# Reading K and V of a decode attention in tiles of four heads instead of two, on one core

## The chip, the core and the metric

The kernel runs on one core of a Trainium2 chip. Its time is the device time of one execution in microseconds (us). TensorE (PE) multiplies matrices, VectorE (DVE), ScalarE (ACT) and GpSimd (POOL) work on elements, SyncE (SP) issues the transfers, and 16 DMA engines carry them from HBM into the 128 partitions of SBUF. PSUM holds TensorE's results, in eight banks of 512 f32 columns.

## The reference

One decode step of one layer for B = 4 sequences with one new token each, model width D = 576, 32 query heads over 16 K/V heads of 128 features, and a window of the last 4096 positions of a cache of 16384:

```python
def _A_ref(x, k_cache, v_cache, wq, wo):
    W = min(4096, max(256, Sk // 4))            # 4096
    rep = Hq // Hkv                             # 2
    q = (x @ wq).reshape(B, Sq, Hq, Dh).transpose(0, 2, 1, 3)
    k = jnp.repeat(k_cache[:, :, Sk - W:, :], rep, axis=1)
    v = jnp.repeat(v_cache[:, :, Sk - W:, :], rep, axis=1)
    p = _softmax(jnp.einsum("bhqd,bhkd->bhqk", q, k) * (Dh ** -0.5), axis=-1)
    o = jnp.einsum("bhqk,bhkd->bhqd", p, v)
    return o.transpose(0, 2, 1, 3).reshape(B, Sq, Hq * Dh) @ wo

h = x + _A_ref(_layernorm(x), A_k_cache, A_v_cache, A_wq, A_wo)
h2 = h + _B_ref(_layernorm(h), B_W_gate, B_W_up, B_W_down)   # relu(x Wg) * (x Wu) @ Wd, F = 4608
```

All inputs are bf16. The windows of K and V are 134 MB of the 159.6 MB that the kernel reads.

## The kernel before

Each engine has a program of its own, written out in order by hand: `prog_sync` (SP's transfers), `prog_pool`, `prog_act`, `prog_dve`, `prog_pe`. `S.op` and `S.dma` add an instruction with the names that it waits for (`deps`) and the name that it signals. An engine takes its instructions strictly in the order of its program, so an instruction that waits holds up all behind it.

**Tiles.** K and V come as "duos": two heads of one sequence, 4096 positions each, 16 KB a partition, 2 MB. Partition 2p + s holds 64 positions of head s. There are 32 duos of K and 32 of V. `add` gives each transfer a place in `pool` and makes it wait for the last reader of what lay there. K has four slots, freed by the second transpose of a duo (`TR`), V has four, freed by its product (`PV`). The order of the transfers is Wq, five duos of K, then K and V in turn (`VLEAD` = 5), Wo, W_gate, W_up, W_down. `pool` is reused for the weights behind: Wo in K's slots, W_gate and W_up where the last V duos lay, W_down in place of Wo, once `ATTN` (the product with Wo) is done.

**Scores.** DVE transposes each half duo in 32 x 32 blocks of f32 words, two bf16 at a time (`tr`, L414), from `pool` into `kT`, a ring of three halves. TensorE (`qk`, all its matmuls have the helper's line L518) multiplies it with `qz`, a query matrix that is zero except for the rows of one duo. Four duos make a batch: their scores add up in the same four banks `sc`, 16 query rows in each of four groups of 32 partitions. Columns alternate between the two heads of a duo, so half of the scores belong to the wrong head.

**Softmax.** After a batch's last score DVE takes the maximum (`rmax`, L417), POOL reduces it over partitions (L293), DVE makes two biases (`fbias`, L425 to L429), one for each head position; for rows of the wrong head the bias is so low that the exponential is 0. ACT takes the exponentials (L342), one instruction for each half and head position, into `P`. DVE transposes `P` (`trp`, L433), ACT casts it to bf16 `prob` (L349).

**Values.** TensorE multiplies `prob` with V (`pv`) into a bank for the batch, ACT copies the bank (`cpy`, L327), TensorE picks the diagonal blocks (`ext`) and DVE divides by the sums (`norm`). `pv` runs five duos behind `qk`.

**Order on DVE.** All transposes of K in turn; after the eighth half of a batch the maximum and the biases; then the first transpose of the next batch, and only then `trp` of this batch. `qk` of the next batch waits for the exponentials (`EXP`), since there is only one set of banks.

The rest (projection of q, Wo, the second layer norm, the gated feed-forward part) is as before and after.

Of the kernel before, what the change touches and what calls it, by code (L numbers as in the profile page):

```python
# [12 lines left out]
B = 4  # L13
# [6 lines left out]
T = WIN // 64  # L20
# [3 lines left out]
NDUO = B * KVH // 2  # L24
NB = 4
NBATCH = NDUO // NB
NHB = 4 * NB
# [3 lines left out]
DUO = 2 * WIN * DH // 128  # L31
NKS = 4
NVS = 4
# [3 lines left out]
NKT = 3  # L37
VLEAD = 5
PVLAG = 5
# [63 lines left out]
def bass_sequential_preLN__sliding_block_cached__glu_gated_reglu__decode_kernel(  # L103
# [12 lines left out]
    with ExitStack() as es:  # L116
# [4 lines left out]

        pool = sb("pool", [128, (NKS + NVS) * DUO], BF16)
        kT = sb("kT", [128, NKT, DUO // 4], FP32)
# [6 lines left out]
        x_f = sb("x_f", [B, D], FP32)  # L130
        junk_f = sb("junk_f", [B, D], FP32)
# [12 lines left out]
        qz = sb("qz", [128, 2, NB, 4, 128], BF16)  # L144
        mask = sb("mask", [128, 3, NHB], FP32)
        selT = sb("selT", [128, 4, NHB], FP32)
        rmx = sb("rmx", [128, 2, 2], FP32)
        rsel = sb("rsel", [128, 2], FP32)
# [4 lines left out]
        bias = sb("bias", [128, 2, 2], FP32)  # L153
        rs2 = sb("rs2", [128, 2, 4], FP32)
        rs1 = sb("rs1", [128, 2], FP32)
        P = sb("P", [128, T * 32], FP32)
        probT = sb("probT", [128, T, 32], FP32)
        prob = sb("prob", [128, 2, NB, T, 4], BF16)
# [12 lines left out]
        hhT = probT[:, 0:FC // 2, :].bitcast(BF16).rearrange("p f b -> p (f b)")[:, 0:FC * 32].rearrange("p (f b) -> p f b", b=32)  # L171
        S8 = probT[:, FC // 2:FC // 2 + 16, :].bitcast(BF16).rearrange("p f b -> p (f b)")
# [39 lines left out]
        def duo(cache, d):  # L212
            b, m = divmod(d, KVH // 2)
            return cache[b, 2 * m:2 * m + 2, SK - WIN:SK, :].rearrange("s (p t) d -> p s (t d)", p=64)

        def add_K(d):
            s = d % NKS
            add(("K", d), f"kslot{s}", s * DUO, DUO, ("TR", 2 * d + 1),
                lambda e, o: e.dma_start(out=o, in_=duo(A_k_cache, d)))

        def add_V(d):
            s = d % NVS
            add(("V", d), f"vslot{s}", (NKS + s) * DUO, DUO, ("PV", d),
                lambda e, o: e.dma_start(out=o, in_=duo(A_v_cache, d)))
# [3 lines left out]
        add(("wq", 0), "wq0", NKS * DUO, 4 * HQ, "QMM",  # L228
            lambda e, o: e.dma_start(out=o, in_=A_wq[0:512, :].rearrange("(p u) n -> p (u n)", u=4)))
        add(("wq", 4), "wq4", NKS * DUO + 4 * HQ, HQ // 2, "QMM",  # L230
            lambda e, o: e.dma_start(out=o, in_=A_wq[512:576, :].rearrange("r (u n) -> (r u) n", u=2)))
        for m in range(NDUO + VLEAD):
            if m < NDUO:
                add_K(m)
            if m >= VLEAD:
                add_V(m - VLEAD)
# [60 lines left out]
        def prog_act(S):  # L297
# [12 lines left out]
            def qzero(n):  # L310
                b, q = divmod(n, 2)
                for g in range(4):
                    deps = []
                    if g == 0:
                        deps = ["D_QR", "QZ0"] if n < 2 else [("QK", 2 * NB * (n - 1) - 1)]
                    src = bass.AP(tensor=qrep, offset=32 * g * 4 * H * B + NHB * q * B + b,
                                  ap=[[4 * H * B, 32], [4 * B, NB], [H * B, 4], [B, 4]])
                    dst = bass.AP(tensor=qz, offset=32 * g * 2 * NB * 512 + (n % 2) * NB * 512 + 32 * g,
                                  ap=[[2 * NB * 512, 32], [512 + 4, NB], [128, 4], [1, 4]])
                    S.op(a, lambda e, src=src, dst=dst: e.copy(out=dst, in_=src), deps=deps,  # L320
                         name=("QZ", n) if g == 3 else None, signal=g == 3)

            def cpy(n):
                deps = [("PV", NB * n + NB - 1)]
                if n >= 2:
                    deps.append(("EXT", n - 2))
# [4 lines left out]
            for n in range(NBATCH):  # L331
# [19 lines left out]
                if n >= 1:  # L351
                    cpy(n - 1)
# [352 lines left out]
```

## Time and profile before

| | before |
|---|---|
| median of the runs (3) | 382.47 us (382.41 to 382.47) |
| the profiled execution: time, span of its instructions | 382.39 us, 381.1 us |
| read from HBM | 159.58 MB, 419 GB/s over the span |
| DMA engines busy | 98.8% of the span |
| PE, DVE, ACT busy | 284.2, 206.3, 53.5 us |
| granted TensorE clock, mean | 0.909 |

A line of a group reads: line, engine, operation, output <- input, partitions x elements and type, count; then busy us and mean ns of one; then the idle time ahead of it and what ended that. A line of a timeline begins with the start and the length in us; several neighbours of a kind are merged, with their count. Durations hold the first to the last element; instructions of an engine can overlap a little.

### The profile page before, as it was taken

How to read it: one execution, taken by the hardware profiler on the slowest of the kernel's cores; microseconds unless marked ns; L12 is line 12 of the kernel's file. 1: busy time of each engine (PE TensorE's matmuls, PEld its weight loads, DVE VectorE, ACT ScalarE, POOL GpSimd, SP SyncE). 2: the span in 40 equal slices, each digit the busy share in tenths (PEclk: the TensorE clock that was granted, in tenths of full speed). 3: DMA queues.
4: the chain of work that ended last, by engine and by line, in shares of the span. 5: the costliest groups of instructions: out<-in, count | busy, mean ns of one | idle time of the engine just before them, and what ended most of it. 6: DMA issues, size and time to landing. Idle time of an engine off the chain costs nothing.

```text
span 381.1 us, 3911 instructions
## 1 busy us (share of the span) xinstructions
PE 284.2 (75%) x1701; PEld 124.4 (33%) x1716; DVE 206.3 (54%) x193; ACT 53.5 (14%) x129; POOL 8.2 (2%) x22
## 2 busy tenths in 40 slices
PE   0059749976996699669957995799779996945474
PEld 0053213322432243224322432243224333435341
DVE  0259789369447754774487548644775443042021
ACT  4012050021102110211031103100310021010020
POOL 4100000000000000000000000000000000000000
PEclk9999969998999899989998999899859997975669
DMA  8999999999999999999999999999999999999995
GB/s 331 409 430 428 426 435 420 434 423 428 431 423 433 423 430 425 428 430 426 430 426 428 430 426 425 432 425 430 426 428 432 421 433 420 420 444 432 414 411 227
DMA packets 11985, 159.84 MB, mean 419 GB/s; under 512 B 1336, under 2 KB 1472, under 8 KB 2624
## 3 DMA queue, kind: packets, MB, share of 16 engines
q1 hardware_dynamic: 11960, 159.59, 98.8%
q8 instruction: 13, 0.21, 0.2%
q14 instruction: 4, 0.03, 0.0%
q10 hardware_dynamic: 8, 0.00, 0.0%
HBM read 159.58 MB, written 0.00 MB: 419 GB/s over the span
## 4 chain that ended last, share of the span: by engine, by line
DMA 34%; PE 33%; DVE 20%; issue 5%; ACT 5%; SPq 1%; POOL 1%; POOLq 0%
DMA pool<-in_A_k_cache_dram 27%; PE pb L518 17%; PE sc L518 16%; DVE kT L414 11%; DMA pool<-in_B_W_down_dram 7%; ACT P L342 4%; DVE probT L433 3%; DVE rmx L417 3%; SPq L254 1%; POOL bcm L293 1%; DVE P L475 1%; DVE P L471 0%; DVE bias L429 0%; DVE sel L374 0%; ACT cp L327 0%
## 5 line engine op out<-in xcount | busy, mean ns | idle before, releaser
L414 DVE STREAM_TRANSPOSE kT<-pool 128x2048 f32<-128x2048 f32 x64 | 144.2, 2290 | 55.8 <-DMA pool<-in_A_k_cache_dram 52.9
L518 PE MATMUL sc<-kT,qz 128*128 128x512 bf16 x497 | 132.1, 418 | 50.2 <-DVE kT L414 46.7
L518 PE MATMUL pb<-pool,prob 128*16 128x512 bf16 x512 | 116.5, 388 | 0.0
L518 PEld LDWEIGHTS sc<-kT,qz 128*128 128x128 bf16 x512 | 48.6, 101 | 130.7 <-DVE kT L414 57.6
L518 PEld LDWEIGHTS pb<-pool,prob 128*16 128x16 bf16 x512 | 43.7, 91 | 70.1 <-issue 16.4
L342 ACT ACTIVATE P<-sc,bias 128x512 f32<-128x512 f32 x32 | 22.2, 720 | 174.9 <-DVE bias L429 174.9
L417 DVE TENSOR_REDUCE rmx<-sc 128x2 f32<-128x2048 f32 x8 | 18.3, 2291 | 32.2 <-PE sc L518 32.2
L433 DVE STREAM_TRANSPOSE probT<-P 128x2048 f32<-128x2048 f32 x8 | 18.5, 2312 | 7.9 <-ACT P L342 7.9
L525 PE MATMUL pb<-ident_b,xn_bf 4*128 4x4 bf16 (+1 forms) x5 | 0.4, 180 | 20.8 <-ACT xn_bf L306 20.8
L327 ACT COPY cp<-pb 128x512 f32<-128x512 f32 x8 | 4.7, 585 | 68.3 <-PE pb L518 68.3
L518 PE MATMUL pb<-selT,cp 128*128 128x16 f32 x64 | 8.6, 267 | 4.3 <-ACT cp L327 4.3
L442 DVE RECIPROCAL rs_sb<-pb 128x32 f32<-128x32 f32 x4 | 1.4, 338 | 18.0 <-PE pb L518 18.0
L349 ACT CAST prob<-probT 128x1024 bf16<-128x1024 f32 x8 | 8.4, 1045 | 19.0 <-DVE rs L436 19.0
L518 PEld LDWEIGHTS pb<-selT,cp 128*128 128x128 f32 x64 | 8.9, 205 | 6.3 <-ACT cp L327 5.3
L505 DVE TENSOR_TENSOR P<-pb,P 128x288 bf16<-128x288 f32 (+1 forms) x2 | 0.8, 402 | 17.5 <-PE pb L518 17.5
L518 PE MATMUL sc<-oX,pool 128*128 128x4 bf16 (+1 forms) x160 | 6.6, 177 | 3.7 <-DVE oX L478 3.7
L293 POOL PARTITION_ALL_REDUCE bcm<-pmax x8 | 3.1, 388 | 290.0 <-DVE pmax L420 290.0
L518 PE MATMUL pb<-pool,hnT 128*32 128x288 bf16 (+1 forms) x48 | 4.4, 408 | 6.4 <-DMA pool<-in_B_W_up_dram 6.4
L320 ACT COPY qz<-qrep 32x64 bf16<-32x64 bf16 x32 | 7.8, 244 | 7.3 <-DVE qrep L451 7.0
L518 PE MATMUL pb<-pool,probT 128*4 128x288 bf16 x72 | 5.7, 285 | 4.0 <-DMA pool<-in_B_W_down_dram 3.4
L518 PE MATMUL sc<-pool,hnT 128*32 128x288 bf16 (+2 forms) x112 | 7.3, 375 | 1.4 <-DMA pool<-in_B_W_gate_dram 1.4
L518 PEld LDWEIGHTS sc<-oX,pool 128*128 128x128 bf16 (+1 forms) x160 | 6.5, 123 | 3.9 <-issue 3.8
(107 smaller groups left out, 79.9 us busy)
## 6 DMA issues: line engine op xcount, KB each, us to landing
pool<-in_A_k_cache_dram SPq DMA_DIRECT2D x32, 2048.0 KB, 28.7
pool<-in_A_v_cache_dram SPq DMA_DIRECT2D x32, 2048.0 KB, 26.3
pool<-in_A_wo_dram SPq DMA_DIRECT2D x4, 1152.0 KB, 21.4
pool<-in_B_W_gate_dram SPq DMA_DIRECT2D x1, 4608.0 KB, 23.9
pool<-in_B_W_up_dram SPq DMA_DIRECT2D x1, 4608.0 KB, 29.4
pool<-in_A_wq_dram SPq DMA_DIRECT2D x1, 4096.0 KB, 13.2
pool<-in_B_W_down_dram SPq DMA_DIRECT2D x2, 1296.0 KB, 22.9
pool<-in_B_W_down_dram SPq DMA_DIRECT2D x5, 432.0 KB, 25.5
```

What stands on the lines that cost most here:

```text
L254: lambda e, g0=g0, g1=g1, j0=j0, nj=nj: e.dma_start(out=wd_sb[:, g0:g1, j0 * D:(j0 + nj) * D], in_=B_W_down[g0 * 128 * JJ:g1 * 128 * JJ, : ...
L293: S.op(g, lambda e, n=n: e.partition_all_reduce(bcm[:, n % 2, :], pmax[:, n % 2, :], 128, bass_isa.ReduceOp.max), deps=deps, name=("PAR", n))
L320: S.op(a, lambda e, src=src, dst=dst: e.copy(out=dst, in_=src), deps=deps, name=("QZ", n) if g == 3 else None, signal=g == 3)
L327: S.op(a, lambda e: e.copy(out=cp[:, n % 2, :], in_=pb[PVB + n % 2]), deps=deps, name=("CP", n))
L342: S.op(a, lambda e, n=n, th=th, u=u: e.activation(out=P[:, th * 1024 + u:(th + 1) * 1024:2], in_=sc[:, th * 1024 + u:(th + 1) * 1024:2], f ...
L349: S.op(a, lambda e, n=n: e.copy(out=prob[:, n % 2, :, :, :], in_=probT[:, :, 0:NHB].rearrange("p t (r x) -> p r t x", x=4)), deps=deps, na ...
L414: S.op(v, lambda e: e.transpose(out=dst, in_=src), deps=deps, name=("TR", i))
L417: S.op(v, lambda e: e.tensor_reduce(out=rmx[:, n % 2, :], in_=sc[:, :].rearrange("p (x u) -> p u x", u=2), axis=AX.X, op=ALU.max), deps=[( ...
L433: S.op(v, lambda e: e.transpose(out=probT[:, :, :].rearrange("p t j -> p (t j)"), in_=P[:, :]), deps=[("EXP", n, 1)] + ([("CMP", n - 1)] i ...
L442: S.op(v, lambda e: e.reciprocal(out=rs_sb[:, b, :], in_=pb[OB][:, 64 + b * H:64 + (b + 1) * H]), deps=[("SUM", b)], name=("RS", b))
L475: S.op(v, lambda e: e.tensor_reduce(out=oS.rearrange("p (x b) -> p x b", b=B), in_=oM.rearrange("p (x s b) -> p x b s", s=8, b=B), axis=AX ...
L518: S.op(t, lambda e: e.matmul(o, lhsT=l, rhs=r, start=start, stop=stop, skip_group_check=skip), deps=deps, name=name, signal=name is not None)
```

## The change

A tile is now a "quad": four heads of one sequence, 32 KB a partition, 4 MB; partition 4p + s holds 128 positions of head s. There are 16 of K and 16 of V, and K and V share one ring of four slots that are taken in the order of the transfers. V runs two quads behind K.

A quad is transposed in four instructions of the old size; its output is sorted by head, so that `qk` can multiply each head's 512 columns with a query matrix for that head alone. The scores of all four heads of two quads (a batch) then add up in one bank for each half, two banks a batch, and batches alternate between two pairs of banks. The maximum runs over 1024 columns. Each exponential reads a whole bank, once for each of the four head positions, each with its bias, and writes bf16 straight into `P`, with the four positions side by side. `trp` transposes bf16 in two halves, right behind `fbias`, into one of two buffers from which `pv` reads; the cast `CMP` is gone. The bank of the products with V now holds a whole sequence (four quads), so `cpy` and `ext` come once a sequence. `qz` is filled for each quad.

Parts of the diff, without what is renamed only; of functions whose old form stands above, mostly the new lines:

```diff
-T = WIN // 64
 F = 4608
 FC = F // 128
 DC = 5
-NDUO = B * KVH // 2
-NB = 4
-NBATCH = NDUO // NB
-NHB = 4 * NB
+NS = 4
+NQUAD = B * KVH // NS
+NPB = KVH // NS
+NB = 2
+NBATCH = NQUAD // NB
+NHQ = 2 * NS
+NHB = NHQ * NB
+TQ = WIN // 32
 SCALE = DH ** -0.5
 EPS = 1e-5
 
-DUO = 2 * WIN * DH // 128
-NKS = 4
-NVS = 4
+QUAD = NS * WIN * DH // 128
+NSLOT = 4
 ROW = 4608
 GU0 = 24064
 NWO = 4
-NKT = 3
-VLEAD = 5
-PVLAG = 5
+NKH = 2
+VLEAD = 2
...
-        pool = sb("pool", [128, (NKS + NVS) * DUO], BF16)
-        kT = sb("kT", [128, NKT, DUO // 4], FP32)
+        pool = sb("pool", [128, NSLOT * QUAD], BF16)
+        kT = sb("kT", [128, NKH, QUAD // 4], FP32)
...
-        P = sb("P", [128, T * 32], FP32)
-        probT = sb("probT", [128, T, 32], FP32)
-        prob = sb("prob", [128, 2, NB, T, 4], BF16)
...
+        Pb = P[:, :].bitcast(BF16).rearrange("p (x s) -> p x s", s=NS)
+        Pw = P[:, :].bitcast(BF16)
+        pT = [probT[:, a, :].bitcast(BF16).rearrange("p (a t h) -> p t a h", t=TQ, h=NHQ) for a in range(2)]
...
+        def quad(cache, i):
+            b, m = divmod(i, NPB)
+            return cache[b, NS * m:NS * m + NS, SK - WIN:SK, :].rearrange("s (p t) d -> p s (t d)", p=32)
+
+        slots = iter(range(2 * NQUAD))
+
+        def add_K(i):
+            x = next(slots) % NSLOT
+            add(("K", i), f"slot{x}", x * QUAD, QUAD, ("TR", 2 * i + 1),
+                lambda e, o: e.dma_start(out=o, in_=quad(A_k_cache, i)))
+
+        def add_V(i):
+            x = next(slots) % NSLOT
+            add(("V", i), f"slot{x}", x * QUAD, QUAD, ("PV", i),
+                lambda e, o: e.dma_start(out=o, in_=quad(A_v_cache, i)))
...
+                for i in range(NB * (n + 1), min(NB * (n + 2), NQUAD)):
+                    qzero(i)
                 for th in range(2):
+                    for u in range(NS):
                         deps = []
                         if th == 0 and u == 0:
                             deps = [("BIAS", n)]
                             if n >= 1:
+                                deps.append(("TRP", n - 1, 1))
                             if n >= 2:
                                 deps.append(("RSUM", n - 2))
                         S.op(a, lambda e, n=n, th=th, u=u: e.activation(
+                            out=Pb[:, th * 512:(th + 1) * 512, u], in_=pb[2 * (n % 2) + th], func=ACT.Exp,
+                            scale=SCALE, bias=bias[:, n % 2, u:u + 1], accum_out=rs2[:, n % 2, NS * th + u:NS * th + u + 1]),
+                            deps=deps, name=("EXP", n, th) if u == NS - 1 else None, signal=u == NS - 1)
+                if n >= 2 and n % 2 == 0:
+                    cpy(n // 2 - 1)
+            cpy(B - 1)
...
-            def tr(i):
-                deps = [land(("K", i // 2))]
-                if i >= NKT:
-                    deps.append(("QK", i - NKT))
-                x0 = at[("K", i // 2)] + (i % 2) * (DUO // 2)
-                src = pool[:, x0:x0 + DUO // 2].bitcast(FP32).rearrange("p (t c k) -> p c t k", c=2, k=32)
-                dst = kT[:, i % NKT, :].rearrange("p (c t k) -> p c t k", c=2, k=32)
-                S.op(v, lambda e: e.transpose(out=dst, in_=src), deps=deps, name=("TR", i))
+            def tr(i, j):
+                f = 2 * i + j // 2
+                deps = [land(("K", i))]
+                if f >= NKH:
+                    deps.append(("QK", f - NKH))
+                x0 = at[("K", i)] + j * (QUAD // 4)
+                src = pool[:, x0:x0 + QUAD // 4].bitcast(FP32).rearrange("p (t c k) -> p c t k", c=2, k=32)
+                dst = kT[:, f % NKH, :].rearrange("p (s c t k) -> p c t k s", s=NS, c=2, k=8)[:, :, (j % 2) * (TQ // 4):(j % 2 + 1) * (TQ // 4), :, :]
+                src = src.rearrange("p c t (k s) -> p c t k s", s=NS)
+                S.op(v, lambda e: e.transpose(out=dst, in_=src), deps=deps, name=("TR", f) if j % 2 else None)
...
+                S.op(v, lambda e: e.tensor_reduce(out=rmx[:, n % 2:n % 2 + 1], in_=sc[:, (n % 2) * 1024:(n % 2 + 1) * 1024], axis=AX.X, op=ALU.max),
...
             def trp(n):
-                S.op(v, lambda e: e.transpose(out=probT[:, :, :].rearrange("p t j -> p (t j)"), in_=P[:, :]),
-                     deps=[("EXP", n, 1)] + ([("CMP", n - 1)] if n >= 1 else []), name=("TRP", n))
+                for th in range(2):
+                    h0, h1 = th * TQ // 2, (th + 1) * TQ // 2
+                    S.op(v, lambda e, h0=h0, h1=h1: e.transpose(out=pT[n % 2][:, h0:h1, :, :], in_=Pw[:, h0 * 32:h1 * 32].rearrange("p (t a h) -> p t a h", a=4, h=NHQ)),
+                         deps=[("EXP", n, th)] + ([("PV", NB * (n - 2) + NB - 1)] if n >= 2 and th == 0 else []), name=("TRP", n, th))
...
+            for i in range(NQUAD):
+                for j in range(4):
+                    tr(i, j)
...
+                if i % NB == NB - 1:
+                    rmax(i // NB)
+                    fbias(i // NB)
+                    trp(i // NB)
+                if i >= NPB + VLEAD and (i - VLEAD) % NPB == 0:
+                    norm((i - VLEAD) // NPB - 1)
...
+            def qk(f):
+                i, th = divmod(f, 2)
+                n, r = divmod(i, NB)
+                kv_ = kT[:, f % NKH, :].bitcast(BF16).rearrange("p (s c x e) -> p s c e x", s=NS, c=2, e=2)
+                deps = [("TR", f)]
+                if th == 0:
+                    deps.append(("QZ", i))
+                if r == 0 and n >= 2:
+                    deps.append(("EXP", n - 2, th))
+                for s in range(NS):
                     for ce in range(4):
+                        last = s == NS - 1 and ce == 3
+                        mm(pb[2 * (n % 2) + th], qz[:, r, s, ce, :], kv_[:, s, ce // 2, ce % 2, :],
+                           r == 0 and s == 0 and ce == 0, r == NB - 1 and last, deps=deps, name=("QK", f) if last else None)
+                        deps = []
...
+            def pv(i):
+                n, a = divmod(i, NB)
+                b, r = divmod(i, NPB)
+                x0 = at[("V", i)]
+                deps = [("TRP", n, 1), land(("V", i))]
+                if r == 0 and b >= 2:
+                    deps.append(("CP", b - 2))
+                for tg in range(TQ // 4):
+                    last = tg == TQ // 4 - 1
+                    mm(pb[PVB + b % 2][32 * r:32 * r + 32, :], pT[n % 2][:, 4 * tg:4 * tg + 4, a, :],
+                       pool[:, x0 + tg * 512:x0 + (tg + 1) * 512], tg == 0, last, deps=deps, name=("PV", i) if last else None)
+                    deps = []
...
+            for i in range(NQUAD + VLEAD):
+                if i < NQUAD:
                     qk(2 * i)
                     qk(2 * i + 1)
+                if i >= VLEAD:
+                    j = i - VLEAD
+                    if j % NPB == 0 and j >= NPB:
+                        ext(j // NPB - 1)
+                    pv(j)
+            ext(B - 1)
```

## The prediction

> **What bounds the kernel now.** I read the page's parts 1 to 3 first, then the groups by line with shapes kept apart, then the timeline of one batch.
>
> ```profile
> span 381.1 us, 3911 instructions
> DMA  8999999999999999999999999999999999999995
> q1 hardware_dynamic: 11960, 159.59, 98.8%
> L414 DVE STREAM_TRANSPOSE kT<-pool 128x2048 f32<-128x2048 f32 x64 | 144.2, 2290 | 55.8 <-DMA pool<-in_A_k_cache_dram 52.9
> ```
>
> The DMA engines are busy 98.8% of the span, and the transposes of K wait 52.9 us for K to land: the kernel is bound by its transfers. From 60 to 320 us the stretch moves 428 GB/s, one 2 MB tile every 4.895 us by its landings in the trace, so eight tiles (four pairs of heads, K and V: one batch) every 39.2 us. One batch of compute:
>
> ```profile
> 153.38 2.29 DVE L417 TENSOR_REDUCE rmx<-sc 128x2 f32<-128x2048 f32 x1 [5.63 <-PE sc L518]
> 155.70 0.17 DVE L420 TENSOR_TENSOR pmax<-mask,rmx 128x16 f32<-128x16 f32 x1
> 156.39 0.17 DVE L425 SCALAR_TENSOR_TENSOR t<-bcm,mask 128x16 f32<-128x16 f32 x1 [0.51 <-POOL bcm L293]
> 156.80 0.23 DVE L429 TENSOR_SCALAR bias<-rsel,bmin 128x2 f32<-128x2 f32 x1
> 157.07 0.72 ACT L342 ACTIVATE P<-sc,bias 128x512 f32<-128x512 f32 x1 [21.51 <-DVE bias L429]
> 159.12 0.72 ACT L342 ACTIVATE P<-sc,bias 128x512 f32<-128x512 f32 x1
> 159.95 2.31 DVE L433 STREAM_TRANSPOSE probT<-P 128x2048 f32<-128x2048 f32 x1 [0.71 <-ACT P L342]
> 162.48 6.69 DVE L414 STREAM_TRANSPOSE kT<-pool 128x2048 f32<-128x2048 f32 x3
> 164.85 3.46 PE L518 MATMUL sc<-kT,qz 128*128 128x512 bf16 x8 [3.57 <-DVE kT L414]
> 190.97 2.29 DVE L417 TENSOR_REDUCE rmx<-sc 128x2 f32<-128x2048 f32 x1 [4.07 <-PE sc L518]
> ```
>
> The reader should see two things. From maximum to maximum (153.38 to 190.97) a batch takes 37.6 us: compute is only 4% ahead of DMA's 39.2, so little extra work on the chain makes compute the bound. And after 3.57 us of idleness TensorE does 8 matmuls in 3.46 us (0.42 each), against 0.227 when it is kept busy (16 in 3.79): its granted clock had dropped to half.
>
> **The change, part by part.**
>
> *Transfers.* Twice the bytes a packet, half as many. The trace's 16 KB packets take 614 ns (median), the one 32 KB transfer's (Wq) 1213, the 36 KB ones (gate, up) 1367. A 4.5 MB weight lands 10.92 us after the one before; between that and 4.895 us for 2 MB a straight line gives 9.715 us for 4 MB, 0.075 saved a tile, 2.4 us over 32 tiles. From the packet medians it is 15 ns x 8 packets x 32 = 3.8. I take 2.4. It is worth something only while DMA is the bound.
>
> *The transposes of K (the term that decides).* Still 64 of 128x2048 f32, but the output now steps: in memory the heads lie outermost, in the order of writing they come innermost, so every 4-byte element is written 4 KB from the last. Before, the output is contiguous. No DVE instruction of this trace writes such steps, so I bound it by these rows:
>
> ```profile
> L475 DVE TENSOR_REDUCE P<-P 128x128 f32<-128x1024 f32 x1 | 2.0, 1961 | 0.0
> L427 DVE TENSOR_REDUCE bmin<-t 128x1 f32<-128x16 f32 x8 | 1.4, 170 | 0.3
> L417 DVE TENSOR_REDUCE rmx<-sc 128x2 f32<-128x2048 f32 x8 | 18.3, 2291 | 32.2 <-PE sc L518 32.2
> L359 ACT ACTIVATE P<-sc 128x216 f32<-128x216 f32 x1 | 0.6, 585 | 0.0
> L359 ACT ACTIVATE P<-sc 128x72 f32<-128x72 f32 x1 | 0.3, 343 | 0.0
> L508 DVE STREAM_TRANSPOSE probT<-P 128x288 bf16<-128x288 bf16 x4 | 1.9, 478 | 0.1
> ```
>
> L417 and L427 give DVE's full rate: (2291-170)/2032 = 1.044 ns an element, 153 ns fixed, and 153 + 2048 x 1.044 is L414's 2290. L475 reads SBUF in steps of 16 bytes: (1961-153)/1024 = 1.77 ns. L359 on ACT writes SBUF in steps of 128 bytes: (585-343)/144 = 1.68 ns. One is the right engine and the wrong side, the other the reverse; both say that single elements in far places cost 1.7 ns. Ends: no effect, 2.29 us; twice DVE's cycle, 153 + 2048 x 2.088 = 4.43. A gain is excluded, since the element count stays. I take the middle of the two rows, 1.72 ns: 153 + 3523 = 3.68 us. Back to back, transposes follow 0.08 sooner than they last (6.69 for three), so 3.60 each.
>
> The Trainium skill, "Vector Engine (DVE) Microarchitecture Reference", section 5.2, speaks directly against this edit: a port keeps full rate only for pairs of adjacent 4-byte words, and an output that hops 4 KiB at every element measured 1.71 ns. No run here shows that for a transpose; by its figure a transpose would be 3.66 us and the sum 1 us lower.
>
> *From the last score to the next transpose.* Before, the next transpose runs ahead of the transpose of P (156.94 before 159.95), so the exponentials are hidden. Now trp(n) is called right behind fbias(n): DVE waits for ACT, and behind that wait are queued the next tile's four transposes, hence TensorE's next scores. Steps: 0.11 to the maximum; maximum over 1024 instead of 2048, 153 + 1069 + 40 = 1.26; to T8 0.69 (POOL's reduction inside); BMIN and BIAS 0.41; to the first exponential 0.27. Exponentials are eight of 128x512 instead of four, 0.685 apart (157.07 to 159.12 is three): 7 x 0.685 + 0.83 (159.12 to 159.95) = 5.63; the first half's transpose fits under the second four. The second half's transpose, 2048 bf16 elements: L508 gives (478-153)/288 = 1.13 ns, at most 2.46, at least 2.24; I take 2.24. RS1, RSUM 0.29. Sum 10.9 us in which DVE moves no K.
>
> *Hidden.* The cast of P (8.4 us of ACT) goes; qz is built in twice as many copies, and its last four (1.0 us) run while DVE finds the maximum (2.7). Scores in two pairs of banks remove TensorE's wait for the exponentials, which DVE's order now replaces. 32 fewer DMA issues on an SP that mostly waits; two memsets and two extra RSEL at the start run before x is normalised. If uncovered, none is over 1 us. norm(b) now stands between two tiles: DVE waits there for the scores (3.48), EXT and SUM (1.0), and itself takes 0.7: 5.2 us, in three places (tiles 6, 10, 14).
>
> *The sum, when DVE sets the pace.* A batch (two tiles): 8 x 3.60 + 0.13 + 16 score matmuls 3.42 + 10.9 = 43.2. TensorE idles 3.7 us ahead of those 16, so its clock is often at half: 0 to 1.7 us, I take 0.9: 44.1. That is 5 us over DMA's 4 x 9.715 = 38.9, so DMA waits, and its 2.4 us gain is lost.
> - First tile landed at 25.0 (before, the second 2 MB tile, 25.1): transpose to 28.7, query copies 1.7 as from 26.04 to 27.74, seven more transposes 25.2, scores 4.4: first batch ends at 60.0.
> - Seven more: 308.7, and three norms 15.6: 384.3.
> - Last probabilities +10.6, two tiles of V at 32 x 0.216 = 7.0 each: 401.9 and 408.9.
> - W_gate may start when V14's slot is free, 401.9 + 1.3 (issue to landing of the tiny output): then gate, up, down, 15.9 MB at 428 GB/s, 37.2: 440.4. ATTN comes 13.6 after the last V product (333.99 to 347.63 before), at 422.5, in time for W_down.
> - The slowest DMA engine's lag and the tail, 2.4 + 2.2 (before 3.4 and 2.2): span 445.0. The profiled execution before took 382.39 with a span of 381.1 (median of the runs 382.47): plus 1.3, **446 us**.
>
> Each 0.1 us on a transpose is 6.4 us of time.
>
> **The rivals.**
>
> *Stepped writes cost nothing (faster).* For it: the reads of L414 already step by block, and its rows show no loss. Against: L475, L359. Then the longest loop is 10.9 + two transposes 4.5 + cold scores 5.1 + scores 3.4 + V 7.0 + two scores 6.8 = 37.7, under 38.9; the ring has four tiles, of which compute holds at most two, so DMA never stops: 382.4 - 2.4 = **380.0**. The point: 8 s + 14.5 + 0.9 and 2.2 for norms (three in seven) reach 38.9 at s = 2.66, so about 2.7 us a transpose decides. Chance 0.17; the margin of 1 us is so thin that 0.02 of it ends unchanged and 0.02 slower.
>
> *Stepped writes cost two DVE cycles or more.* L359's 1.68 ns is 2.2 times ACT's contiguous 0.76 (585 ns for 512 elements, 244 for 64); if the ratio holds rather than the time, a transpose takes 4.43, 64 x 0.75 = 48 more: **494 us**. Chance 0.15.
>
> *HBM.* The heads of a tile lie 4 MB apart, four instead of two. The Trainium skill, "DMA: Bandwidth & Descriptors", section on latency and other measured facts, has row pitches of 4 MiB at half rate or less. The trace disagrees: two heads 4 MB apart stream at 428 GB/s. If four halved it, 134 MB at 214 would take 627 us and the whole some **690**. Chance 0.01.
>
> **How the numbers follow.** Forecast as summed: 0.67, 446 us, of its own 430 to 465 (1.6 to 1.9 ns an element, clock term 0 to 1.7 a batch). With the doubling rival the range reaches 500; milder losses (about 1.5 ns) lower it to 425. That holds 0.8; the free case at 380 stays out. About 0.2% is what a measurement of this kernel can tell from no change. Faster by more: 0.13, the free case alone. Same: 0.02. Slower: 0.85.
>
> **What would show it.** In the profile after: L414's successor (kT<-pool) at a mean near 3.7 us instead of 2.29, some 235 us of DVE; DMA's row with holes from the second quarter on; SP waiting on kT and PE, K landings no longer among DVE's releasers; maxima 43 to 50 us apart; the granted clock below 0.909. A mean of 2.3 there, with DMA still at 9s, makes the prediction wrong by that one term; a mean of 3.7 with a time below 420 would mean that the chain of 10.9 us overlaps more than I think.

## The result and the profile after

| | before | after |
|---|---|---|
| median of the runs | 382.47 us (382.41 to 382.58, 4) | 480.49 us (479.43 to 481.58, 4) |
| after / before | | 1.256 (95% interval 1.253 to 1.260) |
| span of the profiled execution | 381.1 us | 479.9 us |
| DMA engines busy | 98.8% | 79.6% |
| PE, DVE, ACT busy | 284.2, 206.3, 53.5 us | 283.4, 301.4, 103.8 us |
| granted TensorE clock | 0.909 | 0.839 |

The changed kernel is 98 us slower. The page's first parts, then its groups by line:

```profile
span 479.9 us, 3896 instructions
DMA  8999990599859986898199948994689768926996
GB/s 347 429 436 437 436 402 8 216 393 436 355 219 393 436 352 262 350 419 369 44 385 427 421 167 350 433 393 180 262 359 438 341 262 350 384 99 237 422 409 265
L412 DVE STREAM_TRANSPOSE kT<-pool 128x2048 f32<-128x2048 f32 x64 | 229.3, 3704 | 3.6 <-DMA pool<-in_A_k_cache_dram 3.6
L348 ACT ACTIVATE P<-sc,bias 128x512 bf16<-128x512 f32 x64 | 77.5, 1417 | 55.7 <-DVE bias L425 55.7
L431 DVE STREAM_TRANSPOSE probT<-P 128x2048 bf16<-128x2048 bf16 x16 | 37.0, 2312 | 59.6 <-ACT P L348 59.6
```

DMA's row, all 9s before, has holes in every batch; where data flows without a hole it comes at some 436 GB/s. The transposes of K wait 3.6 us for K instead of 52.9: transfers are no longer the bound. They take 3704 ns instead of 2290, and the exponentials (L348) twice as long as before (1417 ns, 720 then), eight a batch instead of four. One batch on DVE, and TensorE's part in it (the timelines; start and length first):

```profile
216.00 2.31 DVE L431 STREAM_TRANSPOSE probT<-P 128x2048 bf16<-128x2048 bf16 x1 [5.03 <-ACT P L348]
220.73 2.31 DVE L431 STREAM_TRANSPOSE probT<-P 128x2048 bf16<-128x2048 bf16 x1 [2.42 <-ACT P L348]
...
223.26 28.64 DVE L412 STREAM_TRANSPOSE kT<-pool 128x2048 f32<-128x2048 f32 x8
255.80 1.23 DVE L415 TENSOR_REDUCE rmx<-sc 128x1 f32<-128x1024 f32 x1 [3.89 <-PE sc L512]
...
258.22 0.23 DVE L425 TENSOR_SCALAR bias<-rsel,bmin 128x4 f32<-128x4 f32 x1
```

```profile
230.88 4.68 PE L512 MATMUL sc<-kT,qz 128*128 128x512 bf16 x15 [15.60 <-DVE kT L412]
237.60 3.79 PE L512 MATMUL sc<-kT,qz 128*128 128x512 bf16 x16 [2.04 <-DVE kT L412]
```

At the top DVE waits 5.03 + 2.42 us for the exponentials of the batch before (L431) while no K moves; then eight transposes take 28.64 us (before, 8 x 2.23 = 17.8), the maximum waits 3.89 us for the scores, and the bias at 258.22 starts the next eight exponentials, with the same two waits behind it. TensorE idles 15.6 us ahead of a batch's first scores (22.2 in the second batch). The 15 listed then take 0.31 us each at a granted clock of 0.74, where 16 kept busy take 0.227 each at 1.00. From maximum to maximum a batch takes 47.5 us, with a normalisation 54.2 to 54.6; before it was 32.5 once and then 37.6 to 40.2, about DMA's pace of 39.2.

### The profile page after: what moved, and what is told of

The parts are those of the page before. It is cut to its first block, busy times and chain, and to the rows that moved or that the text cites. A ratio compares the mean times of both kernels' runs of the same rounds, so it can differ in the third digit from the quotient of the medians.

```text
span 479.9 us, 3896 instructions
## 1 busy us (share of the span) xinstructions
PE 283.4 (59%) x1669; PEld 127.4 (27%) x1684; DVE 301.4 (63%) x201; ACT 103.8 (22%) x213; POOL 8.2 (2%) x22
## 3 DMA queue, kind: packets, MB, share of 16 engines
q1 hardware_dynamic: 7352, 159.59, 79.6%
## 4 chain that ended last, share of the span: by engine, by line
DVE 45%; PE 27%; ACT 16%; DMA 8%; issue 1%; SPq 1%; POOL 1%
DVE kT L412 35%; PE sc L512 17%; ACT P L348 16%; PE pb L512 10%; DMA pool<-in_A_k_cache_dram 5%; DVE probT L431 4%; DMA pool<-in_B_W_down_dram 3%; DVE rmx L415 2%; SPq L259 1%; POOL bcm L298 1%; DVE P L469 0%; DVE pmax L417 0%; DVE bias L425 0%; DVE rowsum L436 0%; DVE t L421 0%
## 5 line engine op out<-in xcount | busy, mean ns | idle before, releaser
L412 DVE STREAM_TRANSPOSE kT<-pool 128x2048 f32<-128x2048 f32 x64 | 229.3, 3704 | 3.6 <-DMA pool<-in_A_k_cache_dram 3.6
L512 PE MATMUL sc<-kT,qz 128*128 128x512 bf16 x497 | 138.0, 437 | 150.6 <-DVE kT L412 149.9
L512 PE MATMUL pb<-pool,probT 128*32 128x512 bf16 (+1 forms) x584 | 119.8, 372 | 10.9 <-DVE rs L434 7.8
L348 ACT ACTIVATE P<-sc,bias 128x512 bf16<-128x512 f32 x64 | 77.5, 1417 | 55.7 <-DVE bias L425 55.7
L431 DVE STREAM_TRANSPOSE probT<-P 128x2048 bf16<-128x2048 bf16 x16 | 37.0, 2312 | 59.6 <-ACT P L348 59.6
L512 PEld LDWEIGHTS pb<-pool,probT 128*32 128x32 bf16 (+1 forms) x584 | 51.3, 96 | 77.6 <-issue 9.1
L325 ACT COPY qz<-qrep 32x32 bf16<-32x32 bf16 x64 | 13.9, 218 | 255.4 <-PE sc L512 244.2
L415 DVE TENSOR_REDUCE rmx<-sc 128x1 f32<-128x1024 f32 x8 | 9.8, 1224 | 35.6 <-PE sc L512 35.6
L348 ACT ACTIVATION_READ_ACCUMULATOR P<-sc,bias 128x1 f32 x64 | 18.8, 295 | 0.0
L512 PEld LDWEIGHTS pb<-selT,cp 128*128 128x128 f32 x32 | 4.1, 191 | 1.7 <-ACT cp L332 1.2
## 6 DMA issues: line engine op xcount, KB each, us to landing
pool<-in_A_k_cache_dram SPq DMA_DIRECT2D x16, 4096.0 KB, 17.8
```

What stands on the lines that cost most here:

```text
L348: S.op(a, lambda e, n=n, th=th, u=u: e.activation(out=Pb[:, th * 512:(th + 1) * 512, u], in_=pb[2 * (n % 2) + th], func=ACT.Exp, scale=SCA ...
L412: S.op(v, lambda e: e.transpose(out=dst, in_=src), deps=deps, name=("TR", f) if j % 2 else None)
L415: S.op(v, lambda e: e.tensor_reduce(out=rmx[:, n % 2:n % 2 + 1], in_=sc[:, (n % 2) * 1024:(n % 2 + 1) * 1024], axis=AX.X, op=ALU.max), dep ...
L431: S.op(v, lambda e, h0=h0, h1=h1: e.transpose(out=pT[n % 2][:, h0:h1, :, :], in_=Pw[:, h0 * 32:h1 * 32].rearrange("p (t a h) -> p t a h", ...
L512: S.op(t, lambda e: e.matmul(o, lhsT=l, rhs=r, start=start, stop=stop, skip_group_check=skip), deps=deps, name=name, signal=name is not None)
```

## The experiments

The theory: two outputs written in steps, K's transposes and the exponentials, stand on DVE's serial chain, and the order in which DVE waits for ACT adds their lengths. Rivals: the transfers of 32 KB a partition or the ring of four slots; TensorE's lost clock; the order alone.

### Write patterns side by side (m1_patterns)

In short form (the f32 exponentials are taken with a scale of 0):

```diff
-    dst = kT[...].rearrange("p (s c t k) -> p c t k s", s=NS, c=2, k=8)...   # all of K's transposes
+    j == 0: contiguous        j == 1: single words 2 KB apart
+    j == 2: pairs of adjacent words, 2 KB apart        j == 3: words 16 bytes apart
-    out=Pb[:, th * 512:(th + 1) * 512, u]                                    # all exponentials
+    Pw[:, 0:512], Pw[:, 0:1024:2], Pw[:, 0:2048:4], Pw[:, 0:4096:8]          # bf16, 2, 4, 8 and 16 bytes apart
+    P[:, 0:512], P[:, 0:1024:2], P[:, 0:2048:4]                              # f32, 4, 8 and 16 bytes apart
+    Pw[:, 0:2048] as (x s b), s=4, b=2, [s = 1]                              # pairs of bf16, 16 bytes apart
```

> One look at writing patterns, each on a line of its own; the output is not the reference's, since scores and probabilities land in other places. Transposes of 128x2048 f32 in the changed kernel took 3704 ns, with every 4-byte word written 4 KB from the last. Theory (single far words cost the writing port 1.7 ns): contiguous output 2290, words 2 KB apart 3650 to 3750, pairs of adjacent words 2 KB apart 2290 to 2350 (the Trainium skill's granule rule), words 16 bytes apart 3700 or more. Rival (the number of dimensions of the pattern costs, not the distance): pairs cost as much as single words. Exponentials of 128x512 took 1417 ns with 2-byte elements 8 bytes apart, 720 before with 4-byte elements 8 bytes apart. Theory A (a write must fill at least half of a 16-byte line's words): 2-byte elements next to each other 720, 4 bytes apart 720, 8 and 16 bytes apart 1400; 4-byte elements next to each other and 8 bytes apart 720, 16 bytes apart 1400; 2-byte pairs 16 bytes apart 1400. Theory B (2-byte elements cost as such): all four 2-byte patterns 1400, all 4-byte ones 720. Theory C (PSUM read without a step costs): all 1400.

The groups by line of its one run, in the order of the diff:

```profile
L427 DVE STREAM_TRANSPOSE kT<-pool 128x2048 f32<-128x2048 f32 x16 | 36.8, 2299 | 2.6 <-DMA pool<-in_A_k_cache_dram 2.2 <-PE sc L536 0.3
L429 DVE STREAM_TRANSPOSE kT<-pool 128x2048 f32<-128x2048 f32 x16 | 58.7, 3669 | 0.0
L432 DVE STREAM_TRANSPOSE kT<-pool 128x2048 f32<-128x2048 f32 x16 | 36.3, 2271 | 0.0
L435 DVE STREAM_TRANSPOSE kT<-pool 128x2048 f32<-128x2048 f32 x16 | 60.3, 3771 | 0.0
L349 ACT ACTIVATE P<-sc,bias 128x512 bf16<-128x512 f32 x8 | 5.5, 687 | 50.9 <-DVE bias L449 50.9
L351 ACT ACTIVATE P<-sc,bias 128x512 bf16<-128x512 f32 x8 | 6.6, 830 | 0.3
L353 ACT ACTIVATE P<-sc,bias 128x512 bf16<-128x512 f32 x8 | 11.2, 1401 | 0.3
L355 ACT ACTIVATE P<-sc,bias 128x512 bf16<-128x512 f32 x8 | 20.2, 2525 | 0.3
L357 ACT ACTIVATE P<-sc,R_sb 128x512 f32<-128x512 f32 x8 | 5.5, 687 | 0.3
L359 ACT ACTIVATE P<-sc,R_sb 128x512 f32<-128x512 f32 x8 | 5.7, 709 | 0.3
L361 ACT ACTIVATE P<-sc,R_sb 128x512 f32<-128x512 f32 x8 | 9.2, 1156 | 0.3
L363 ACT ACTIVATE P<-sc,bias 128x512 bf16<-128x512 f32 x8 | 5.7, 709 | 0.3
```

A transpose pays for single words without a neighbour, whether 2 KB apart (3669 against 2299) or 16 bytes (3771), and nothing for pairs (2271), so it isn't the number of dimensions that costs. On ACT the cost grows with the step, and for 2-byte elements it starts earlier: 830 ns at 4 bytes, 1401 at 8, 2525 at 16, where f32 takes 687 without a step, 709 at 8 and 1156 at 16. Pairs of bf16 at 16 bytes cost next to nothing (709). None of the three theories for ACT fits all of these rows: A has 1400 for single bf16 at 16 bytes and for pairs, B 1400 for every bf16 pattern, C 1400 for all. Why ACT is slow here stays open; the rows are prices. The changed kernel's exponentials are the row of single bf16 at 8 bytes.

### Each step taken back (e1_flat_k, e2_flat_exp)

```diff
-                dst = kT[:, f % NKH, :].rearrange("p (s c t k) -> p c t k s", s=NS, c=2, k=8)[...]
+                dst = kT[:, f % NKH, (j % 2) * 2048:(j % 2 + 1) * 2048].rearrange("p (c t k) -> p c t k", c=2, k=32)
```

> The changed kernel, but the transposes of K write without steps (the scores then mix the heads, so the result is another one). Theory (two terms: stepped transposes, and a DVE that waits 15 us a batch from the last score to the next transpose): transposes 2290 ns; then TensorE's loop sets the pace, 15.0 + two transposes 4.5 + cold scores 5.5 + scores 3.4 + V 7.0 + two scores 6.8 = 42.2 a batch, over DMA's 38.9; time 405 to 415 us. Rival 1 (the transposes alone): DMA is the bound again, 380 to 383 us. Rival 2 (the ring of four large slots starves DMA by itself): above 450 us.

427.87 us (ratio 1.115, 1.111 to 1.120). The transposes are back at 2279 ns and the time falls by 52.6 us, but a batch still takes 43.4 to 45.1 us: DVE now waits for TensorE's scores and for the exponentials.

```profile
L411 DVE STREAM_TRANSPOSE kT<-pool 128x2048 f32<-128x2048 f32 x64 | 142.3, 2279 | 13.6 <-PE sc L511 10.1
```

The expectation had the kind of the loop right and the time 13 to 23 us too short. About 7 us of that are the 32 scores after the idle time: they stay at 0.31 us each, 9.84 in a batch where 8.9 had been taken. The rest was not broken down.

```diff
-                            out=Pb[:, th * 512:(th + 1) * 512, u], in_=pb[2 * (n % 2) + th], func=ACT.Exp,
+                            out=Pw[:, (NS * th + u) * 512:(NS * th + u + 1) * 512], in_=pb[2 * (n % 2) + th], func=ACT.Exp,
```

> The changed kernel, but each exponential writes its 512 bf16 results next to each other (the probabilities then lie in other places, so the result is another one). Theory: 0.685 us from one to the next instead of 1.175, eight in a row on the path of each of eight batches: 8 x 8 x 0.49 = 31 us less, 449 us. Rival (ACT is off the path, DVE's transposes alone set the pace): 478 to 481 us.

447.35 us (1.168, 1.164 to 1.172), 33.1 less than the changed kernel and 1 from the prediction's own sum, which had taken the exponentials at about this pace. That it comes so close is partly luck: from the first maximum to the last it is 2 us shorter than the sum has, and its start, its last products with V and its tail are 3 us longer. An exponential takes 698 ns, and DVE's two waits for ACT shrink:

```profile
246.39 2.31 DVE L431 STREAM_TRANSPOSE probT<-P 128x2048 bf16<-128x2048 bf16 x1 [2.85 <-ACT P L348]
249.06 2.31 DVE L431 STREAM_TRANSPOSE probT<-P 128x2048 bf16<-128x2048 bf16 x1 [0.37 <-ACT P L348]
```

### The order alone (e3_order)

```diff
+                if i % NB == 0 and i > 0:
+                    trp(i // NB - 1)          # behind the next tile's four transposes
                 if i % NB == NB - 1:
                     rmax(i // NB)
                     fbias(i // NB)
-                    trp(i // NB)
+                if i == NQUAD - 1:
+                    trp(NBATCH - 1)
```

> The changed kernel, but DVE transposes the whole next tile of K before it transposes the probabilities, as the kernel before did with half a tile. Theory: the 9.6 us of exponentials run under 14.5 us of transposes; a batch is 29.0 + 3.5 + 2.8 + 4.9 = 40.2 us on DVE instead of 47.5, three of them 6.7 more; time 420 to 430 us. Rival (the wait moves to TensorE, which needs the probabilities for V): 460 us or more.

421.90 us (1.101, 1.097 to 1.105): 58.6 us come back with both stepped writes in place. The transposes of P wait 7.4 us in the whole run instead of 59.6. What is left is the wait for the scores, 41.4 us in the run:

```profile
227.35 1.23 DVE L415 TENSOR_REDUCE rmx<-sc 128x1 f32<-128x1024 f32 x1 [5.25 <-PE sc L515]
```

### The step in the kernel before (e6_before_hop)

```diff
-                dst = kT[:, i % NKT, :].rearrange("p (c t k) -> p c t k", c=2, k=32)
+                dst = kT[:, i % NKT, :].rearrange("p (s c t k) -> p c t k s", s=4, c=2, k=8)
+                src = src.rearrange("p c t (k s) -> p c t k s", s=4)
```

> The kernel before, its transposes of K alone made to write each word 2 KB from the last (the scores then stand in another order of columns than the values, so the result is another one). Theory (the step costs 1.4 us a transpose, but what that does depends on what waits): 64 x 1.4 = 90 us more DVE work; a batch on DVE is 8 x 3.62 + 3.8 for the scores + 2.3 + 1.3 + 2.3 + 0.4 = 39.1, about DMA's 39.2, since the exponentials run under a transpose: 384 to 395 us. Rival (stepped transposes alone account for the slow kernel): 440 us or more.

404.64 us (1.057, 1.053 to 1.061).

```profile
L415 DVE STREAM_TRANSPOSE kT<-pool 128x2048 f32<-128x2048 f32 x64 | 232.2, 3724 | 1.2 <-PE sc L519 1.2
```

The same 64 stepped transposes cost the kernel before 22 us, where taking them out of the changed kernel gave 52.6. In the kernel before, DVE idled 55.8 us ahead of its transposes, nearly all of it for K to land; in e6 that is 1.2, so these waits took up most of the 88 us that the transposes grew by. (What remains, 33 us, is more than the 22 measured; it was not broken down.) The time is 10 us above the expected range: from the third batch on the maximum waits 4.8 to 5.3 us for the scores where 3.8 had been taken, and a batch takes 40.5 to 41.1 us from the fourth on instead of 39.1.

### Nothing but the transfers left (e9_flat_k_order)

The two edits of e1 and e3 together.

> The changed kernel with K's transposes writing without steps (which puts wrong keys into the scores: part of the computation is changed) and with the transpose of P moved behind the next tile's four transposes. What is left of the change is its transfers of 4 MB, its ring of four slots and the exponentials' stepped writes. Theory (both costs lie on DVE's chain, and nothing in the transfers is slow): a batch of DVE and TensorE is 9.1 + 4.6 + 15 + 2.6 = 31 us by the transposes of 2.28 us, so DMA's 38.9 us a batch is the bound again: 379 to 383 us, DMA busy over 97%, DVE waiting for K to land. Rival (a ring of four 4 MB slots runs dry, or the tail after the last V has a hole): DMA under 95%, over 386 us.

380.23 us (0.994, 0.992 to 0.996), DMA's row all 9s again, at 431 GB/s from 60 to 320 us where the kernel before has 428. The transposes wait for K again:

```profile
L411 DVE STREAM_TRANSPOSE kT<-pool 128x2048 f32<-128x2048 f32 x64 | 142.3, 2281 | 51.2 <-DMA pool<-in_A_k_cache_dram 49.9
```

The theory holds: transfers of 4 MB and the ring of four slots cost nothing, and the time falls by 2.4 us by the medians of the same session (1.4 to 2.9 by the interval), the gain that the prediction had at 2.4. Beside e3 this run also prices the step in K's transposes once the transpose of P stands later: 421.90 - 380.23 = 41.7 us.

### Pairs of adjacent words (e4_pairs, e5_pairs_order, e12_pairs_near)

m1 says that pairs are free on both engines, so a complete kernel could keep the step. Partition 8a + 2s + b holds positions of head s, which makes neighbours of one head adjacent; each tile comes in two transfers, one to the even and one to the odd partitions. Of the diff, the transfers alone:

```diff
-            return cache[...].rearrange("s (p t) d -> p s (t d)", p=32)
+            return cache[...].rearrange("s (a b t) d -> b a s (t d)", a=16, b=2)
-    make(e, pool[:, off:off + n])
+    make(e, pool[b::2, off:off + n], b)       # b = 0, 1
+    # e12: "s (b a t) d -> b a s (t d)"       e5, e12: with the order of e3
...
```

> The changed kernel with another order of partitions in a tile: positions in pairs (partition 8a + 2s + b holds positions of row 2a + b of head s), so that transposes write pairs of adjacent words and exponentials pairs of adjacent 2-byte elements; each tile is two transfers of 64 partitions. Theory: transposes 2290 and exponentials 709 ns as in the single patterns measured; from the last score to the next transpose 10.9 us as first summed; TensorE's loop as with flat transposes (43.9 a batch) less 4.0 = 39.9, still a little over DMA's 38.9; 32 us under that run's 428: 392 to 400 us. Rival (with both steps gone DMA is the bound): 379 to 383 us. Rival (transfers to every other partition are slow): above 400 us.

> The pairs, and DVE transposes the whole next tile of K before the probabilities. Theory: TensorE's loop falls to about 30 us and DVE's to 30 a batch, DMA's 38.9 is the bound again, and the 32 KB packets show what they are worth: 2.4 us (3.8 by the packets' medians) under the kernel before: 379 to 381 us. Rival (the ring of four large slots starves DMA): 385 us or more, with SP waiting and holes in DMA's row. Rival (packets gain nothing): 382 to 383.

> The kernel with pairs of adjacent words and the later transpose of P, complete, with one thing changed: each of a tile's two transfers to every other partition reads, of every head, 16 pieces of 32 KB that lie next to each other in HBM (512 KB in one run) instead of every second piece of 1 MB. Theory (the half rate comes from writing every other partition): nothing changes, 32 KB packets near 2.4 us, 216 to 222 GB/s, 660 to 690 us. Rival (it comes from skipping every other piece in HBM): packets near 1.2 us, over 425 GB/s, and with transposes of 2.28 us and exponentials of 0.73 DMA is the bound: 379 to 383 us.

e4 took 680.58 us (1.775, 1.767 to 1.783); e5 a median of 674.64 and e12 of 676.96 (their runs spread from 624 to 693, so no ratio is given). The page of e4:

```profile
GB/s 339 215 216 216 215 216 216 220 219 224 220 224 217 224 237 220 231 228 224 225 225 221 222 227 218 219 218 216 220 219 216 218 218 216 221 222 234 444 411 253
L416 DVE STREAM_TRANSPOSE kT<-pool 128x2048 f32<-128x2048 f32 x64 | 142.4, 2281 | 284.0 <-DMA pool<-in_A_k_cache_dram 284.0
L352 ACT ACTIVATE P<-sc,bias 128x512 bf16<-128x512 f32 x64 | 43.9, 725 | 77.2 <-DVE bias L429 77.2
```

The compute part came as expected (2281 and 725 ns), but the last rival of e4 came true: K and V arrive at half rate (221 GB/s from 60 to 600 us, 222 in e12), and only the weights at the end, which go to all partitions, come at 444 GB/s. A 32 KB packet takes 2393 ns (median) instead of 1213. e12 reads each head's pieces in one run and its packets stay at 2382 ns, so skipping in HBM is not the cause. Whether it is the step over partitions or that a transfer has 64 of them was not separated. What e4 and e5 were meant to show of the order with neither step is hidden by the slow transfers.

### The step read by TensorE (e7_pe_step)

```diff
+    # transposes as in e1, order as in e3
-    kv_ = kT[...].rearrange("p (s c x e) -> p s c e x", s=NS, c=2, e=2)
+    kv_ = kT[...].rearrange("p (j c x s e) -> p s c e j x", s=NS, j=2, c=2, e=2)
...
```

> DVE writes the transposes without steps, heads interleaved, and TensorE reads each head's scores operand in steps of 16 bytes instead; the next tile is transposed before the probabilities; the result is the reference's. Theory 1 (TensorE's moving operand is free to step): 0.23 us a score matmul, DMA-bound, 379 to 382 us. Theory 2 (it reads at half rate): 0.43 us, 64 x 0.43 + 64 x 0.22 + 1 = 42.6 us a batch on TensorE, 400 to 412 us.

692.24 us (1.807, 1.803 to 1.812); neither case was near. TensorE reads its 512 columns 16 bytes apart, and 16 matmuls take 14.58 us, one every 0.90 instead of 0.227:

```profile
224.26 14.58 PE L514 MATMUL sc<-kT,qz 128*128 128x512 bf16 x16
```

It isn't the clock: they start 0.90 us apart at a granted clock of 1.00 (100 to 110 us) as at 0.50 (300 to 310 us).

### A complete kernel with the step (e10_late_max, e11_tail)

e10 puts the maximum and the bias behind the first two transposes of the next tile, and the transpose of P behind its last two.

```diff
                 for j in range(4):
                     tr(i, j)
+                    if j == 1 and i % NB == 0 and i > 0:
+                        rmax(i // NB - 1)
+                        fbias(i // NB - 1)
...
+                if i % NB == 0 and i > 0:
+                    trp(i // NB - 1)
-                if i % NB == NB - 1:
-                    rmax(i // NB)
-                    fbias(i // NB)
-                    trp(i // NB)
+                if i == NQUAD - 1:
+                    rmax(NBATCH - 1)
+                    fbias(NBATCH - 1)
+                    trp(NBATCH - 1)
```

> The changed kernel, complete, in another order on DVE: the maximum and the bias of a batch stand behind the first two transposes of the next tile, the transpose of P behind its last two. No stepped write is taken away. Theory (the waits for the scores and for the exponentials are what made DVE the bound; without them a batch is 8 x 3.65 + 2.7 + 4.7 = 36.6 us on DVE, under DMA's 38.9): 380 to 386 us, waits of the maximum for TensorE under 5 us in all, DMA over 96% busy, no difference from the kernel before that exceeds 1%. Rival (stepped writes are too dear in any order, DVE stays the bound): 395 to 415 us, DVE over 85% busy between 60 and 330 us and SP waiting on the transposes.

395.83 us (1.034, 1.031 to 1.037). By its numbers the rival came: the time, a DVE that is 92% busy from 60 to 330 us, and SP waiting 99 us for the transposes of K. DMA's share says otherwise. Two windows (length; busy us of PE, its weight loads, DVE, ACT and POOL with their instructions; granted clock, DMA's share, GB/s):

```profile
60.00:330.00 270.00, 217.44 (x896) 89.39 (x910) 247.45 (x129) 82.30 (x167) 3.11 (x8) 0.92 0.99 423
330.00:366.00 36.00, 23.14 (x169) 11.88 (x167) 9.88 (x10) 11.18 (x18) 0.00 (x0) 0.85 0.74 304
```

From 60 to 330 us the theory's mechanism is there: DMA is 99% busy, the maximum waits 5.2 us in all for the scores, and the maxima come 38.4 to 39.0 us apart from the third to the seventh. Most of the loss is at the end, where nothing follows to hide the last batch's chain: DVE ends its last transposes at 321.8, the scores end at 326.9, the exponentials at 339.3, the V products at 356.5 (339.9 in e9), and W_gate (350.5) and W_up (356.5) can start only as the V products free their places. e11 shortens this end only:

```diff
+    # K14 and K15 one place earlier among the transfers; W_gate and W_up in two transfers each,
+    # at another place in pool (GU0 = 20736)
+    # norm() one tile later, behind that tile's transposes
+            for h in range(2):                       # V of the last batch by halves of its positions
+                for j in (NQUAD - 2, NQUAD - 1):
+                    pv(j, range(h * TQ // 8, (h + 1) * TQ // 8))
```

> The kernel with the late maximum, complete, changed at its end only: the last two K tiles are transferred one place earlier, each normalisation stands behind the next tile's transposes, the last batch's V products start on the first half of its probabilities (tiles 14 and 15 by halves), and the gate and up weights come in two transfers each. Theory (the late-maximum kernel's loss lies at its end: with K's last landing at 302.6 the V products ended at 356.5, against 339.9 in the kernel with unstepped transposes, and the DMA engines had a hole there): V products end near 347, 9 to 10 us earlier, and with the 34.5 us of compute behind them the time is 381 to 386 us. Rival (the end is not what costs; DVE is short all the way): V products end later than 353 and the time stays over 391 us.

385.65 us (1.008, 1.006 to 1.009). V products end at 345.6, 10.9 earlier, and 10.2 us of time come back; the theory holds. How much each of its edits gives was not separated. DVE is 91% busy from 60 to 330 us here too, so a full DVE isn't what e10 lost by. What remains against e9 (5.4 us) is for the most part a hole at 67 to 86 us, with 330 GB/s instead of 427: DVE can't start before the first tile lands at 25 us, and the fifth K tile then waits for a slot (in e10 until 72.5 us, in e9 until 60.9) that the third tile's transposes free.

```profile
GB/s 328 437 422 437 437 434 425 363 300 407 435 437 437 437 428 430 420 415 434 437 437 435 437 437 427 425 427 427 423 435 438 437 429 434 397 433 426 415 420 213
```

No complete version beat the kernel before.

## Why the prediction was right, and where its sum was short

The forecast was 446 us in a range of 425 to 500; the runs gave 480.5. Its direction and its mechanism held: stepped transposes and a DVE that waits for ACT make DVE's chain the bound, and DMA waits. One term of the sum was too small, 10.9 us a batch where 15.0 were measured. That 480.5 still lies in the range is luck: it lies outside the 430 to 465 that the forecast gave its own sum, and the range reached 500 only through the doubling rival, whose mechanism is not what happened.

One reading of the kernel before was off. It is right that DMA was the bound, but of the 37.6 us between the two maxima, which the prediction takes for compute's own pace, DVE waits 8.7 us for K to land:

```profile
172.61 4.50 DVE L414 STREAM_TRANSPOSE kT<-pool 128x2048 f32<-128x2048 f32 x2 [3.43 <-DMA pool<-in_A_k_cache_dram]
182.39 4.50 DVE L414 STREAM_TRANSPOSE kT<-pool 128x2048 f32<-128x2048 f32 x2 [5.28 <-DMA pool<-in_A_k_cache_dram]
```

The first interval, in which no transpose waits for K, is 32.5 us (45.28 to 77.77). So compute was more than 4% ahead, which is part of why e6 costs 22 us and not 88. The prediction's sum doesn't use this reading. Term by term:

- **Transfers.** Right: 32 KB packets 1213 ns, worth 2.4 us in e9 as forecast, and lost in the changed kernel, where DMA waits.
- **Transposes of K.** Right: 3704 ns against 3.68 us, and 28.64 us for eight, 3.58 each, against 3.60. m1 confirms the middle of the two rows, 1.72 ns a word, over the ends of 2.29 and 4.43 us. The figure of the Trainium skill's "Vector Engine (DVE) Microarchitecture Reference", section 5.2, 1.71 ns, is what a transpose shows too: (3669 - 153) / 2048 = 1.72 in m1, and 1.73 in the changed kernel. Its rule that pairs of adjacent words are free shows as well (2271 against 2299).
- **From the last score to the next transpose.** This step failed. It costed eight exponentials at 0.685 us from one to the next, the pace of the kernel before, whose f32 words also stand 8 bytes apart; the diff makes ACT write 2-byte elements at that step. No row of the page before shows that pattern. What it did show (L359, f32 words 128 bytes apart, 1.68 ns an element against 0.76) is that ACT can pay for a stepped output, and it was used for DVE alone. The exponentials come 1.18 us apart, so the step is 15.0 us instead of 10.9, and it stands eight times in the sum: 8 x 4.1 = 33 us, about the 35 that are missing. e2 gives the same by the reverse: without ACT's step, the last score to the next transpose takes 10.8 us, and 33.1 us come back.
- **Normalisations.** 6.7 to 7.1 us instead of 5.2: the wait is 4.9 instead of 4.5, and the maximum behind it then waits 5.2 to 5.5 instead of 3.9.
- **Batch and sum.** The first batch's scores end at 59.1 (60.0 forecast). A plain batch is 47.5 instead of 44.1, the last scores come at 412.2 instead of 384.3, the V products end at 442.3 instead of 408.9. From there to the end it is 37.6 us against 36.1. A plain batch grew by 3.4 and not by 4.1 since other terms were too large: from the last transpose to the maximum it is 3.9 us, and the sum has 0.13 + 3.42 + 0.9 for TensorE's clock.
- **TensorE's lost clock.** It was not taken away alone. In the batch shown, the 15 scores after the idle time take 4.68 us instead of 15 x 0.227 = 3.4, but DVE's eight transposes run on beside them without a gap, so this delays nothing there. Behind a normalisation the maximum waits 1.3 to 1.6 us longer, and in the last of these batches the trace has the slow scores for it: 16 take 5.39 us after 3.34 us of idleness, instead of 3.79.
- **The rivals.** Free stepped writes are out by m1. Doubling was nearer to the measured time than the forecast, but not by its mechanism: transposes did not double, exponentials did. Its own sum is also not what it says: a ratio of 2.2 would make a transpose 153 + 2048 x 1.044 x 2.2 = 4.86 us, and 4.43 is a ratio of 2. Four stretches of 1 MB, 4 MB apart, stream at 431 GB/s in e9, so the HBM rival is out for this pattern.
- **Cover.** The casts of P that go (8.4 us of ACT) did not show, as forecast; ACT's busy time nevertheless grew by 50 us, and that of the exponentials by 55 (77.5 against 22.2).

The three costs overlap, so their shares don't add: taking back the step in K gives 52.6 us, the step in P 33.1, the order 58.6, and K's step and the order together give back all 100. The early transpose of P without either step was not measured, so what the order costs by itself is open.

## What to carry to other kernels

When a layout change moves sorting into the outputs of DVE or ACT, cost every instruction that writes through the new step, on each engine, at the step's own rate; look for pairs of adjacent words first. Look for a wait for another engine in front of a queue of bulk work: here the transposes of P waited 59.6 us, and moving them gave 58.6. A longer operation costs less where it fills a wait: the same 88 us of longer transposes cost 22 in the kernel before, 41.7 in the changed one with the transpose of P moved, and 52.6 in the changed one as it is. The order of P's transpose is thus only part of the difference. And when a kernel is made transfer-bound again, look at its last batch, whose chain nothing covers.

## What the runs showed of the hardware that was not expected

- ACT's price of a stepped output depends on the step, on the size of an element and on whether it has a neighbour: in m1, 512 bf16 take 687 ns side by side, 1401 at 8 bytes and 2525 at 16, as pairs at 16 bytes 709; f32 takes 709 at 8 bytes and 1156 at 16. Four bytes every 16 thus cost 709 ns as two bf16, and 1156 as one f32.
- TensorE reading its moving operand in 16-byte steps takes 0.90 us for 512 columns instead of 0.227, at a granted clock of 0.50 as at 1.00 (e7).
- Transfers of 32 KB pieces to every other partition, 64 a transfer, run at 221 to 222 GB/s (60 to 600 us of e4, e5 and e12) instead of 431 (60 to 320 us of e9); the order of the pieces in HBM makes no difference.
